# The first loads of a fused attention and MLP kernel reordered, and the taps of its convolution decoded one round later

## The chip, the cores and the metric

The kernel runs on one core of one Trainium2 chip. The metric is the device time of one execution in microseconds (us). PE is the matrix engine, DVE the vector engine, ACT the scalar engine, POOL GpSimd and SP the engine that issues nearly all DMAs; each works through its own instructions in order.

## What is computed

Three blocks follow each other: attention with features of exponentials, an MLP gated by a short convolution, and a second MLP with a low-rank mix along the sequence. B = 4, H = 8, S = 576, D = 64.

```python
def phi(x):                                   # w_phi: 64 x 128
    proj = np.einsum('bhsd,df->bhsf', x, w_phi)
    proj = proj - np.max(np.abs(proj), axis=-1, keepdims=True)
    return np.concatenate([np.exp(proj), np.exp(-proj)], axis=-1)
q_p, k_p = (phi(q), phi(k))
kv = np.einsum('bhsf,bhsd->bhfd', k_p, v); z = np.sum(k_p, axis=2)
num = np.einsum('bhsf,bhfd->bhsd', q_p, kv)
den = np.einsum('bhsf,bhf->bhs', q_p, z)[..., None] + 1e-06
x = num / den                                 # heads put side by side
h = np.maximum(x @ w_in, 0.0)
for k in range(3):                            # conv_w: 3 taps x 1024 channels
    conv_out += conv_w[k][None, None, :] * hp[:, k:k + S, :]   # hp: h, padded
x = h * (1.0 / (1.0 + np.exp(-conv_out))) @ w_out
u = x + low-rank mix of x                     # U, V
out = u + np.maximum(u @ w_ch1, 0.0) @ w_ch2
```

q, k, v and w_phi come as 32-bit floats; the taps `conv_w` and the MLP weights come as 64-bit floats and are decoded on the chip.

## The kernel before, in words

The attention stage runs in eight rounds (`NU`) of four heads each. A round's k and q come in three parts (g = 0 to 2). `centred` (line 256) projects a part with the weights `w2` into PSUM (`ppk`, `ppq`; a pool `ps_p` of two buffers), DVE takes the largest magnitude (`mk`, `mq`, line 266) and subtracts it (`dk`, `dq`, line 268). ACT then makes both exponentials (`ek`, lines 277 and 278). PE forms `kvp` (line 313) in two halves, u = 0 and u = 1, and the sums `zp`; q's features are transposed (`tq`) and exponentiated (`et`). The products `np` (line 381) and `dp` of a round are made during the next one, after ACT has copied `kv` (line 355).

The list `front` (line 480) is the order of a round. PE, DVE and ACT execute in exactly the order in which the code is written (`manual_schedule`); SP and POOL get an order from the tile scheduler. A lag of 1 or -1 in the list means that the step is for the next or the previous round; so `loads_kv` and `loads_q` load one round ahead.

Beside the attention each round decodes two pieces of the later weights (`win00`, `win01`, then `win10`, ...) from 64-bit floats in `split_steps`: a DMA into a staging tile `raw`, two DVE steps (lines 78 and 81), two ACT steps (87 and 89), two DVE steps (97 and 100), a POOL product (101), an ACT copy (171) and two POOL steps (172 and 173). The last of these, line 173, still reads `raw`. The pool `stage` (line 61) has two buffers for each of its tags `raw` and `x`.

The taps go the same way through `load_small` (line 104) at once: DMA, lines 78, 81, 87, 89, 97, 100, 101 and 125, and `load_cw` copies the result to `cw` (line 138). They are first used in the second stage, after 190 us. In the kernel before, `load_cw` is called ahead of the rounds, and its three DMAs gather single 8-byte values, since the taps lie in DRAM as 3 x 1024.

Ahead of all that, `ident` is built by POOL and eight warm-up products (line 230) run on it.

Of the kernel before, what the change touches and what calls it, by code (L numbers as in the profile page):

```python
# [8 lines left out]
F32 = mybir.dt.float32  # L9
# [3 lines left out]
AF = mybir.ActivationFunctionType  # L13
# [5 lines left out]
P = 128  # L19
# [5 lines left out]
def kernel(  # L25
# [15 lines left out]
    nc = tc.nc  # L41

    B, H, S, D = 4, 8, 576, 64
# [5 lines left out]
    NJ = FF // P  # L49
# [8 lines left out]
    cpool = ctx.enter_context(tc.tile_pool(name="cpool", bufs=1))  # L58
# [8 lines left out]
    cw = cpool.tile([P, 3 * NJ], F32, name="cw")  # L67
# [8 lines left out]
    def widen_head(raw, x):  # L76

        nc.vector.tensor_scalar(
            x, raw[:, :, 1], 3, 0x3FFFFFFF, op0=ALU.logical_shift_left, op1=ALU.bitwise_and
        )  # L80
        nc.vector.scalar_tensor_tensor(
            out=x, in0=raw[:, :, 1], scalar=-0x40000000, in1=x, op0=ALU.bitwise_and, op1=ALU.bitwise_or
        )

    def square_and_low(raw):
        high = raw.bitcast(F32)[:, :, 1]
        nc.scalar.activation(high, high, AF.Square)
        low = raw.bitcast(F32)[:, :, 0]
        nc.scalar.activation(low, raw.bitcast(U32)[:, :, 0], AF.Copy, scale=2.0**-52)

    def widen_rest(raw, x, mul_engine):


        low = raw.bitcast(F32)[:, :, 0]
        high = raw.bitcast(F32)[:, :, 1]
        xf = x.bitcast(F32)
        nc.vector.scalar_tensor_tensor(
            out=xf, in0=high, scalar=MIN_NORMAL_HI * MIN_NORMAL_HI, in1=xf, op0=ALU.is_ge, op1=ALU.mult
        )
        nc.vector.tensor_scalar(raw[:, :, 1], x, -0x800000, None, op0=ALU.bitwise_and)  # L100
        mul_engine.tensor_mul(low, low, high)
        return xf, low

    def load_small(p, n, name, parts, zero=()):

        wide = parts[0][2].dtype != F32
        x = stage.tile([P, 512], I32 if wide else F32, tag="x", name=f"{name}_x")[0:p, 0:n]
        if wide:
            raw = stage.tile([P, 512, 2], I32, tag="raw", name=f"{name}_raw")[0:p, 0:n, :]
        for z in zero:  # L110
            nc.gpsimd.memset(raw[:, z, :] if wide else x[:, z], 0)
        for r, c, src in parts:
            a = src.shape[1] if len(src.shape) == 3 else None
            if wide:
                d, s_ = raw[r, c, :], src.bitcast(I32)
                d = d.rearrange("p (a b) t -> p a (b t)", a=a) if a else d.rearrange("p b t -> p (b t)")
            else:
                d, s_ = x[r, c], src
                d = d.rearrange("p (a b) -> p a b", a=a) if a else d
            nc.sync.dma_start(out=d, in_=s_)  # L120
        if wide:
            widen_head(raw, x)
            square_and_low(raw)
            x, low = widen_rest(raw, x, nc.gpsimd)
            nc.vector.tensor_add(x, x, low)
        return x

    everything = slice(0, P)

    def load_cw():  # L130
        f = load_small(
            P, 3 * NJ, "cw",
            [
                (everything, slice(t * NJ, (t + 1) * NJ), conv_w[t : t + 1, :].rearrange("o (j p) -> p j o", p=P))
                for t in range(3)
            ],
        )
        nc.vector.tensor_copy(cw, f)

    def load_us(odd):  # L140
# [81 lines left out]
    G = 3  # L222
    GC = G * P

    w2 = cpool.tile([P, P], F32, name="w2")
    nc.sync.dma_start(out=w2[0:D], in_=w_phi)
    nc.sync.dma_start(out=w2[D:P], in_=w_phi)
    warm = ps_s.tile([P, 512], F32, tag="s", name="warm")
    for i in range(8):
        nc.tensor.matmul(warm[:, 0:P], lhsT=ident, rhs=ident, start=True, stop=True)  # L230
# [9 lines left out]
    def load_part(nm, src, i, g):  # L240
        t = fpool.tile([P, GC], F32, tag=f"{nm}r", name=f"{nm}r{i}_{g}", bufs=4)
        nc.sync.dma_start(out=t, in_=src[i, :, g * GC : (g + 1) * GC])
        raw[nm, i, g] = t

    def loads_kv(i):
        for g in range(G):
            load_part("k", k, i, g)
        t = fpool.tile([P, 10, 2, D], F32, tag="v", name=f"v{i}")
        nc.sync.dma_start(out=t.rearrange("p t h d -> p (t h d)"), in_=v[i])
        raw["v", i] = t  # L250

    def loads_q(i):
        for g in range(G):
            load_part("q", q, i, g)

    def centred(nm, i, g):
# [214 lines left out]
    def step(f, *args):  # L471
        return lambda i: f(i, *args)
# [4 lines left out]
    def second(i):  # L477
# [26 lines left out]
        (first, 0),  # L504
        (step(q_centred, 0), 0),
        (loads_kv, 1),
        (step(kv, 0), 0),
        (step(q_centred, 1), 0),
        (loads_q, 1),
        (step(turn_q, 0), 0),  # L510
        (step(q_features, 0), 0),
# [13 lines left out]
    ]  # L525

    loads_kv(0)
    loads_q(0)
    load_cw()
    att_order, rounds_order = ExitStack(), ExitStack()  # L530
    att_order.enter_context(tc.manual_schedule(engines={mybir.EngineType.PE}))
    rounds_order.enter_context(tc.manual_schedule(engines={mybir.EngineType.DVE, mybir.EngineType.Activation}))
    for i in range(NU):
        for step, lag in front:
            if 0 <= i + lag < NU:
                step(i + lag)
    rounds_order.close()
    i = NU - 1
    for _ in range(4):
# [191 lines left out]
    for n in range(B * NJ):  # L731
        b, j = divmod(n, NJ)
# [227 lines left out]
```

## Time and profile before

| | us |
|---|---|
| three runs, median (lowest, highest) | 830.88 (827.99, 832.11) |
| the profiled execution, device time | 833.57 |
| its span, first to last instruction | 831.5 |
| PE busy (share of the span) | 801.8 (96%) |
| DVE busy | 539.0 (65%) |
| ACT busy | 360.9 (43%) |
| POOL busy | 122.0 (15%) |
| mean granted TensorE clock | 0.989 of full |

Busy times are sums over the whole span; which engine limits a stretch is read from a table by stretches and from the waits in it. A granted clock of 1.00 is 2.4 GHz, 0.50 is 1.2 GHz. "Idle before <- X" in a row of a timeline names the event that ended an engine's idle time. The whole attention stage takes about the first 200 us.

### The profile page before, as it was taken

How to read it: one execution, taken by the hardware profiler on the slowest of the kernel's cores; microseconds unless marked ns; L12 is line 12 of the kernel's file. 1: busy time of each engine (PE TensorE's matmuls, PEld its weight loads, DVE VectorE, ACT ScalarE, POOL GpSimd, SP SyncE). 2: the span in 40 equal slices, each digit the busy share in tenths (PEclk: the TensorE clock that was granted, in tenths of full speed). 3: DMA queues.
4: the chain of work that ended last, by engine and by line, in shares of the span. 5: the costliest groups of instructions: out<-in, count | busy, mean ns of one | idle time of the engine just before them, and what ended most of it. 6: DMA issues, size and time to landing. Idle time of an engine off the chain costs nothing.

```text
span 831.5 us, 12728 instructions
## 1 busy us (share of the span) xinstructions
PE 801.8 (96%) x5092; PEld 647.1 (78%) x5092; DVE 539.0 (65%) x842; ACT 360.9 (43%) x642; POOL 122.0 (15%) x119
## 2 busy tenths in 40 slices
PE   5999999989989999999889999999999999999997
PEld 4666666657879888998668787888888888888886
DVE  3777777876799986985354596894378267231322
ACT  2777777776477664474311242442143132111110
POOL 0144444454331330000000000000000000000000
PEclk7999999999999999999999999999999999999999
DMA  7345555320312010111520221321031020000122
GB/s 209 129 126 170 170 170 170 110 81 2 94 52 102 26 58 26 39 52 38 178 89 1 63 58 45 100 70 34 1 102 51 1 68 34 0 1 1 68 84 76
DMA packets 39435, 61.27 MB, mean 74 GB/s; under 512 B 10257, under 2 KB 24721, under 8 KB 39377
## 3 DMA queue, kind: packets, MB, share of 16 engines
q1 hardware_dynamic: 39376, 60.46, 23.0%
q8 instruction: 40, 0.66, 0.3%
q14 instruction: 19, 0.15, 0.1%
HBM read 50.34 MB, written 10.04 MB: 73 GB/s over the span
## 4 chain that ended last, share of the span: by engine, by line
PE 83%; DVE 8%; DMA 4%; ACT 2%; issue 1%; SPq 1%; POOL 0%; DVEq 0%; ACTq 0%; POOLq 0%
PE po L856 22%; PE hps L834 22%; PE hp L590 10%; PE x2p L638 8%; PE kvp L313 4%; PE np L381 4%; PE ppq L263 2%; PE ppk L263 2%; PE zp L327 2%; PE tq L293 2%; PE dp L406 2%; DVE cv L602 1%; DVE xl L449 1%; PE x2m L654 1%; DMA c_5r<-in_moe_w_ch_dram 1%
## 5 line engine op out<-in xcount | busy, mean ns | idle before, releaser
L840 ACT ACTIVATE hh<-hps 128x512 fp32r<-128x512 f32 (+1 forms) x80 | 44.2, 553 | 214.2 <-PE hps L834 209.6
L841 DVE SCALAR_TENSOR_TENSOR hl<-hps,hh 128x512 fp32r<-128x512 f32 (+1 forms) x80 | 50.6, 633 | 99.2 <-ACT hh L840 99.0
L590 PE MATMUL hp<-xh,win 128*128 128x288 f32 x512 | 105.9, 297 | 0.5 <-ACT h L598 0.5
L638 PE MATMUL x2p<-wout,g 128*128 128x512 f32 x384 | 96.0, 392 | 2.1 <-DVE g L610 1.1
L834 PE MATMUL hps<-uh,c1h 128*128 128x512 f32 (+1 forms) x240 | 88.8, 370 | 1.1 <-ACT uh L796 1.1
L590 PEld LDWEIGHTS hp<-xh,win 128*128 128x128 f32 x512 | 85.1, 190 | 5.2 <-ACT h L598 0.7
L834 PE MATMUL hps<-ul,c1h 128*128 128x512 f32 (+1 forms) x240 | 88.5, 369 | 0.1
L834 PE MATMUL hps<-uh,c1l 128*128 128x512 f32 (+1 forms) x240 | 88.3, 368 | 0.0
L856 PE MATMUL po<-c2h,hh 128*128 128x512 f32 x216 | 84.9, 393 | 0.0
L856 PE MATMUL po<-c2l,hh 128*128 128x512 f32 x216 | 84.8, 393 | 0.0
L861 DVE TENSOR_TENSOR u<-u,po 128x512 f32<-128x512 f32 x90 | 58.5, 680 | 38.2 <-PE po L856 38.2
L856 PE MATMUL po<-c2h,hl 128*128 128x512 f32 x216 | 82.6, 392 | 0.0
L638 PEld LDWEIGHTS x2p<-wout,g 128*128 128x128 f32 x384 | 69.8, 188 | 15.9 <-DVE g L610 1.9
L590 PE MATMUL hp<-xl,win 128*128 128x288 f32 x256 | 76.6, 299 | 2.3 <-DVE xl L449 2.3
L602 DVE SCALAR_TENSOR_TENSOR cv<-h,cw,cv 128x576 f32<-128x576 f32 x64 | 53.3, 835 | 12.1 <-ACT cv L600 11.4
L631 POOL CAST ghold<-g 128x128 fp32r<-128x128 f32 x32 | 31.3, 983 | 155.9 <-DVE g L610 145.9
L834 PEld LDWEIGHTS hps<-uh,c1h 128*128 128x128 f32 x240 | 45.2, 188 | 9.1 <-ACT uh L796 1.3
L590 PEld LDWEIGHTS hp<-xl,win 128*128 128x128 f32 x256 | 48.7, 190 | 4.3 <-DVE xl L449 3.4
L834 PEld LDWEIGHTS hps<-ul,c1h 128*128 128x128 f32 x240 | 45.2, 188 | 8.3 <-DVE ul L797 0.5
L834 PEld LDWEIGHTS hps<-uh,c1l 128*128 128x128 f32 x240 | 45.2, 188 | 7.9
L856 PEld LDWEIGHTS po<-c2h,hl 128*128 128x128 f32 x216 | 41.0, 190 | 8.7
L856 PEld LDWEIGHTS po<-c2l,hh 128*128 128x128 f32 x216 | 41.0, 190 | 8.2
(488 smaller groups left out, 1500.5 us busy)
## 6 DMA issues: line engine op xcount, KB each, us to landing
v<-in_v_dram SPq DMA_DIRECT2D x8, 640.0 KB, 5.6
kr<-in_k_dram SPq DMA_DIRECT2D x24, 192.0 KB, 3.7
qr<-in_q_dram SPq DMA_DIRECT2D x24, 192.0 KB, 3.6
rb<-recd SPq DMA_DIRECT2D x32, 144.0 KB, 3.3
u<-x2d SPq DMA_DIRECT2D x18, 256.0 KB, 4.0
out_dram<-u SPq DMA_DIRECT2D x18, 256.0 KB, 2.1
x2d<-x SPq DMA_DIRECT2D x14, 256.0 KB, 2.3
c_0r<-in_moe_w_ch_dram SPq DMA_DIRECT2D x2, 512.0 KB, 4.2
```

The source lines that it names most:

```text
L263: nc.tensor.matmul(pp[:, s, c], lhsT=x[r, c], rhs=w2[r, :], start=True, stop=True)
L313: nc.tensor.matmul(o[s * D : (s + 1) * D, :], lhsT=raw["v", i][:, 5 * u + n, s, :], rhs=k_tile(i, s, 4 * u + n), start=(n == 0), stop=(n = ...
L381: nc.tensor.matmul(ps[r, 0:HC], lhsT=st["kv"][:, u, a, r], rhs=st["et"][:, s, a, cs], start=(a == 0), stop=(a == 1))
L590: nc.tensor.matmul(ps[:, 0:HC], lhsT=win[kk][:, wi, j * P : (j + 1) * P], rhs=xs[b][kk][xi][:, cs], start=(i == 0), stop=(i == 3 * NK - 1),)
L602: nc.vector.scalar_tensor_tensor(out=cv, in0=h[:, t : t + S], scalar=cw[:, t * NJ + j : t * NJ + j + 1], in1=cv, op0=ALU.mult, op1=ALU.add,)
L631: nc.gpsimd.tensor_copy(ghold[:, :, j, off : off + LEFT], g.bitcast(F32)[:, :, rest : rest + LEFT])
L638: nc.tensor.matmul(x2p[t], lhsT=g[:, gi, ts_], rhs=w[wi], start=(j == 0 and i == 0), stop=(j == NJ - 1 and i == 2),)
L834: nc.tensor.matmul(ps[:, 0:w], lhsT=ch[j, 0][wi][:, kc], rhs=x[:, kk, :], start=(n == 0), stop=(n == 3 * NK - 1))
L840: nc.scalar.activation(hh, ps[:, 0:w], AF.Relu)
L841: nc.vector.scalar_tensor_tensor(out=hl, in0=ps[:, 0:w], scalar=0.0, in1=hh.bitcast(F32), op0=ALU.max, op1=ALU.subtract)
L856: nc.tensor.matmul(po[i][t], lhsT=x[:, cs], rhs=w, start=(j == js[0] and n == 0), stop=(j == js[-1] and n == 2))
L861: nc.vector.tensor_add(u, u, p)
```

## The change

Four edits. The host writes `w_phi` twice below itself, so that one DMA, issued by ACT, fills `w2`; the host also lays the taps out as 128 x 24, so that one DMA of whole rows brings them. The first part of q is loaded ahead of v, in every round. A 128 x 1 tile of zeros goes through ACT's exponential at the beginning. And `load_cw` is called at the end of the first round's list instead of ahead of the rounds.

```diff
     def load_cw():
-        f = load_small(
-            P, 3 * NJ, "cw",
-            [
-                (everything, slice(t * NJ, (t + 1) * NJ), conv_w[t : t + 1, :].rearrange("o (j p) -> p j o", p=P))
-                for t in range(3)
-            ],
-        )
+        f = load_small(P, 3 * NJ, "cw", [(everything, slice(0, 3 * NJ), conv_w)])
         nc.vector.tensor_copy(cw, f)
...
     w2 = cpool.tile([P, P], F32, name="w2")
-    nc.sync.dma_start(out=w2[0:D], in_=w_phi)
-    nc.sync.dma_start(out=w2[D:P], in_=w_phi)
+    nc.scalar.dma_start(out=w2, in_=w_phi)
+    warm_exp = cpool.tile([P, 1], F32, name="warm_exp")
+    nc.gpsimd.memset(warm_exp, 0.0)
+    nc.scalar.activation(warm_exp, warm_exp, AF.Exp)
...
     def loads_kv(i):
         for g in range(G):
             load_part("k", k, i, g)
+        load_part("q", q, i, 0)
         t = fpool.tile([P, 10, 2, D], F32, tag="v", name=f"v{i}")
...
     def loads_q(i):
-        for g in range(G):
+        for g in range(1, G):
             load_part("q", q, i, g)
...
     loads_kv(0)
     loads_q(0)
-    load_cw()
...
         for step, lag in front:
             if 0 <= i + lag < NU:
                 step(i + lag)
+        if i == 0:
+            load_cw()
...
+        elif name == "w_phi":
+            a = _np.concatenate([a, a])
+        elif name == "moe_conv_w":
+            a = _np.ascontiguousarray(a.reshape(3, -1, 128).transpose(2, 0, 1)).reshape(128, -1)
```

DVE, from its first instruction on, in the kernel before. `mk0_1` is `mk` of round one (counted from 0 in names), part 1; the last number of a name is a running number.

```order
L266 TENSOR_REDUCE mk0_0_175<-ppk0_0_168 128x6
L268 TENSOR_TENSOR dk0_0_177<-ppk0_0_168,mk0_0_175 128x768
L78 TENSOR_SCALAR cw_x_150<-cw_raw_151 128x24
L81 SCALAR_TENSOR_TENSOR cw_x_150<-cw_raw_151,cw_x_150 128x24
L266 TENSOR_REDUCE mk0_1_189<-ppk0_1_182 128x6
L268 TENSOR_TENSOR dk0_1_191<-ppk0_1_182,mk0_1_189 128x768
L97 SCALAR_TENSOR_TENSOR cw_x_150<-cw_raw_151,cw_x_150 128x24
L100 TENSOR_SCALAR cw_raw_151<-cw_x_150 128x24
L266 TENSOR_REDUCE mk0_2_203<-ppk0_2_196 128x6
L125 TENSOR_TENSOR cw_x_150<-cw_x_150,cw_raw_151 128x24
L268 TENSOR_TENSOR dk0_2_205<-ppk0_2_196,mk0_2_203 128x768
L138 COPY cw_74<-cw_x_150 128x24
```

DVE at the end of round one and the beginning of round two, in the changed kernel (line numbers are those of the changed code).

```order
L263 TENSOR_REDUCE mq0_2_282<-ppq0_2_275 128x6
L265 TENSOR_TENSOR dq0_2_284<-ppq0_2_275,mq0_2_282 128x768
L97 SCALAR_TENSOR_TENSOR win00x_197<-win00r_196,win00x_197 128x512
L100 TENSOR_SCALAR win00r_196<-win00x_197 128x512
L78 TENSOR_SCALAR cw_x_327<-cw_raw_328 128x24
L81 SCALAR_TENSOR_TENSOR cw_x_327<-cw_raw_328,cw_x_327 128x24
L97 SCALAR_TENSOR_TENSOR cw_x_327<-cw_raw_328,cw_x_327 128x24
L100 TENSOR_SCALAR cw_raw_328<-cw_x_327 128x24
L125 TENSOR_TENSOR cw_x_327<-cw_x_327,cw_raw_328 128x24
L132 COPY cw_74<-cw_x_327 128x24
L263 TENSOR_REDUCE mk1_0_346<-ppk1_0_339 128x6
L265 TENSOR_TENSOR dk1_0_348<-ppk1_0_339,mk1_0_346 128x768
```

The six steps of the taps have moved from between round one's k parts to between `win00` and round two's first k part, now in one block.

SP in the kernel before, at the loads that it issues ahead for rounds two and three, with the semaphores that each waits for.

```order
L242 DMA qr2_0_509<-in_q_dram 128x384 [waits DMAHW7_49,PE_49]
L242 DMA kr2_1_481<-in_k_dram 128x384 [waits DMAHW0_49,PE_49]
L163 DMA win10r_430<-in_moe_w_in_dram 128x1024 [waits DMAHW1_49,DVE_49,Pool_49]
L242 DMA kr2_2_483<-in_k_dram 128x384 [waits DMAHW2_49,PE_49]
L242 DMA kr3_0_747<-in_k_dram 128x384 [waits DMAHW3_49,PE_49]
```

SP in the changed kernel, at the same place.

```order
L238 DMA qr2_0_485<-in_q_dram 128x384 [waits DMAHW3_49,PE_49]
L238 DMA kr2_1_481<-in_k_dram 128x384 [waits DMAHW4_49,PE_49]
L120 DMA cw_raw_328<-in_moe_conv_w_dram 128x48 [waits DMAHW5_49,DVE_49,Pool_49]
L157 DMA win10r_430<-in_moe_w_in_dram 128x1024 [waits DMAHW6_49,DMAHW5_49,DVE_49]
L238 DMA kr2_2_483<-in_k_dram 128x384 [waits DMAHW7_49,PE_49]
```

The load of the taps stands where that of `win10` stood and waits for DVE and POOL as that did; `win10` stands behind it and waits for the taps. ACT's two steps for the taps stand between its copy of `zt` and its copy of `kv`, and POOL's product behind line 173 (line 167 of the changed code) of `win00`. PE's order is the same in both kernels.

## Rows read from the trace of the kernel before

**Rows 1.** The page, busy time, share of the span and instructions of PE.

```profile
PE 801.8 (96%) x5092; PEld 647.1 (78%) x5092; DVE 539.0 (65%) x842; ACT 360.9 (43%) x642; POOL 122.0 (15%) x119
```

**Rows 2.** Stretches: us, busy of each engine, granted clock, DMA share, GB/s.

```profile
8.50:29.80 21.30, 14.03 (x136) 9.03 (x132) 12.13 (x20) 11.18 (x17) 0.23 (x1) 0.76 0.70 210
29.80:51.20 21.40, 21.40 (x244) 13.96 (x240) 16.67 (x23) 15.82 (x29) 7.15 (x6) 1.00 0.40 125
```

**Rows 3.** Timeline of PE, 0 to 30 us: start, us, instructions, idle before.

```profile
1.47 3.43 PE L230 MATMUL warm<-ident 128*128 128x128 f32 x16 [1.47 <-POOL ones L235]
4.82 1.61 PE L263 MATMUL ppk<-w,kr 64*128 64x128 f32 x24
7.86 0.94 PE L263 MATMUL ppk<-w,kr 64*128 64x128 f32 x12 [1.43 <-DVE dk L268]
16.07 1.65 PE L263 MATMUL ppq<-w,qr 64*128 64x128 f32 x12 [7.27 <-DVE dk L268]
17.65 4.23 PE L313 MATMUL kvp<-ek,v 128*64 128x256 f32 x20
21.81 0.94 PE L263 MATMUL ppq<-w,qr 64*128 64x128 f32 x12
...
23.49 2.38 PE L313 MATMUL kvp<-ek,v 128*64 128x256 f32 x20
```

**Rows 4.** Timeline of all engines, 0 to 30 us: loads and the taps.

```profile
0.74 0.60 SPq L226 DMA_DIRECT2D w<-in_w_phi_dram  x1
...
5.48 6.26 SPq L120 DMA_DIRECT2D cw_raw<-in_moe_conv_w_dram  x3
...
6.80 0.96 DVE L268 TENSOR_TENSOR dk<-ppk,mk 128x768 f32<-128x768 f32 x1
...
13.67 1.28 ACT L89 ACT_TABLE_LOAD   x1 [13.67 <-DMA cw_raw<-in_moe_conv_w_dram]
13.71 0.18 DVE L78 TENSOR_SCALAR cw_x<-cw_raw 128x24 int32<-128x24 int32 x1 [5.95 <-DMA cw_raw<-in_moe_conv_w_dram]
...
14.97 0.23 ACT L89 ACTIVATE cw_raw<-cw_raw 128x24 f32<-128x24 uint32 x1
...
17.43 0.23 POOL L101 TENSOR_TENSOR cw_raw<-cw_raw 128x24 f32<-128x24 f32 x1 [15.79 <-DVE cw_raw L100]
```

**Rows 5.** Stretches of 1 us in the front, columns as in rows 2.

```profile
9.80:10.80 1.00, 0.00 (x0) 0.00 (x0) 0.00 (x0) 0.00 (x0) 0.00 (x0) 1.00 0.81 89
...
12.80:13.80 1.00, 0.00 (x0) 0.00 (x0) 0.09 (x1) 0.13 (x1) 0.00 (x0) 0.50 1.01 201
```

**Rows 6.** Timeline of all engines, 28 to 60 us: round two begins.

```profile
29.77 0.94 PE L263 MATMUL ppk<-w,kr 64*128 64x128 f32 x12
...
30.00 1.04 POOL L101 TENSOR_TENSOR win00r<-win00r 128x512 f32<-128x512 f32 x1 [12.35 <-ACT et L302]
...
30.75 0.96 DVE L266 TENSOR_REDUCE mk<-ppk 128x6 f32<-128x768 f32 x1 [0.88 <-PE ppk L263]
...
31.78 0.38 PE L362 MATMUL pz<-ident,zt 128*128 128x128 f32 x2
...
32.35 1.29 POOL L173 TENSOR_TENSOR win<-win00x,win00r 128x512 fp32r<-128x512 f32 x1
...
33.67 0.33 SPq L163 DMA_DIRECT2D win10r<-in_moe_w_in_dram  x1
...
34.18 0.94 PE L263 MATMUL ppk<-w,kr 64*128 64x128 f32 x12
```

**Rows 7.** DMA issues of the whole run: count, KB each, median us to landing.

```profile
w<-in_w_phi_dram SPq DMA_DIRECT2D x2, 32.0 KB, 2.1
cw_raw<-in_moe_conv_w_dram SPq DMA_DIRECT2D x3, 8.0 KB, 5.8
us_raw<-in_moe_U_dram SPq DMA_DIRECT2D x2, 16.0 KB, 3.3
```

**Rows 8.** Answer for the tile `cw_raw`: landing of its three loads.

```profile
DMA to landing us min/median/max: 5.1/5.8/6.8
```

## The prediction

> **What bounds the kernel now.** I read the engines' busy times first: PE is busy 801.8 of 831.5 us [rows 1], so time can only be won where PE stands still or runs slowly. Then the stretches by round of the attention stage: from round two on PE is busy through all of its 21.4 us at full clock, while in the first 30 us it is busy for 14.0 of 21.3 us at a mean granted clock of 0.76 [rows 2]. The change touches only this front, so what matters is when round two begins and at what pace; everything behind is a chain that moves as a block.
>
> The PE timeline of the front shows the hole: after the third group of k it stands idle for 7.27 us, until 16.07, released by a `dk` of DVE [rows 3]. DVE itself stood: its instruction for the taps (`cw_x`, line 78) begins at 13.71, 5.95 us after it was free, because the three loads of the taps had been issued from 5.48 on and took until then [rows 4]. The hole has a second price: the granted clock is still 1.00 at 9.8 to 10.8, but 0.50 (1.2 GHz) at 12.8 to 13.8 [rows 5]. The first group of q therefore takes 1.65 us where the next takes 0.94, and the first half of `kvp` 4.23 us where the second takes 2.38 [rows 3]: 0.71 + 1.85 = 2.56 us.
>
> **Part 1: w in one load on ACT's queue, k first on SP's.** SP gets rid of two issues of 0.6 us [rows 4], and k comes 1.2 us earlier. This buys nothing: the eight warm-up products run from 1.47 to 4.90, and the first group of k starts right there, at 4.82 [rows 3]. They wait for the identity, which POOL builds; POOL gets one more memset before it, so I add 0.1 us. If this cover were gone, the parts together could give up to 1.2 us.
>
> **Part 2: an exponential of zeros.** It draws the 1.28 us table load to the beginning [rows 4], beside the warm-up products. In the kernel before that load ran while DVE was still in `mk` and `dk`, and PE waited for `dk`: no gain. In the changed kernel it keeps 1.28 us off the first exponentials; these are needed by `kvp` at about 10.8, and even 1.28 us later they would end at 7.9 + 1.28 + 1.6 = 10.8. Zero either way.
>
> **Part 3: first q ahead of v.** The first q is needed at 9.9, v at 10.8; by then both are issued and landed in either order (all loads of round one are issued by some 4 us instead of 5.4). Zero.
>
> **Part 4: the taps leave the front.** The DVE order has `mk` and `dk` of the second k part directly behind those of the first. `dk` begins at 6.80 and takes 0.96 [rows 4]; with 0.1 of delay and two more steps of 0.98 the second `dk` ends at 9.85, and the first group of q starts at 9.9 instead of 16.07: 6.15 us. From there PE has no gap: each later DVE step is done when PE comes to it (the first `dq` ends at 13.8, its transposes start at 13.97). Without the long idle I take the clock to stay up, as it did through the 1.43 us wait at 7.86 [rows 3, 5]: another 2.56 us. Round two's first group of k then starts 8.7 us earlier, at 21.1 instead of 29.77 [rows 6].
>
> **Part 5: the taps come back at the end of round one.** This is the step that decides. Only two staging buffers exist for raw data, and both are taken by `win00` and `win01`. The taps' load needs the buffer of `win00`, so SP waits until POOL has done its last step on it: line 173, which ends at 32.35 + 1.29 = 33.64, 3.87 us after round two's first group of k began at 29.77 [rows 6]. In the kernel before it is `win10` that waits there, needed by nobody soon: it is issued at 33.67 [rows 6]. Now it is the taps, and DVE, which works in written order, stands in front of them with `mk` and `dk` of round two behind; ACT too, with the copy of `kv` behind. This chain keeps its distances whatever the front does, because POOL's last step hangs on DVE's line 100 and that on round one's last `dq`.
>
> The length of the wait. The transfer is not in the trace in this shape (128 rows of 192 B). Nearest rows: 2.1 us for the 32 KB halves of w, 3.3 us for the 16 KB pieces of `us_raw`, 5.8 us for the old loads of the taps in 8-byte pieces [rows 7]. I take 2.2, for w has whole rows as the new load has, and keep 1.8 to 3.8 for the range. The Trainium skill, page "DMA: Bandwidth & Descriptors", section on the anatomy of one DMA, puts a DMA at a fixed 2.0 us plus bytes over 436 GB/s (fitted on GpSimd's path), an estimate of 2.06 us for 24.6 KB; the sum would be 0.14 us better by it. The trace agrees for w (2.1) and not for the smaller `us_raw` (3.3).
>
> Counted from round two's first group of k: issue at 3.9, landed at 6.1, then the decode, one step behind the other: six DVE steps of 0.18 to 0.2 us, an ACT step of 0.2 and a POOL step of 0.23 with two hand-overs [rows 4], 1.9 us. DVE is free for `mk` at 8.0 (before: 0.98), `dk` ends at 9.97, and the second group of k starts at 10.05; before it started at 34.18, which is 4.41 [rows 6]. **Loss: 5.64 us.** PE can do `np` meanwhile, but first ACT has to pass its two steps for the taps and copy `kv`: 6.1 + 0.4 (DVE) + 0.4 + 0.6 + 0.2 = 7.7. PE's last work before that is `pz`, which ends 2.4 us after the first group of k [rows 6], so it stands idle for some 5.3 us. In the front the clock had fallen within 3 us of idling (from 8.80; 1.00 until 10.8) [rows 5], so I expect it to fall here and to take about the same 2.56 us from the first `np` and the group behind it. From then on PE is full again as in rounds two to eight: DVE works 16.7 of 21.4 us there [rows 2] and catches up.
>
> **The sum.** Gain 6.15 + 2.56 = 8.7; loss 5.64 + 2.56 = 8.2. Net 0.5 us faster: 833.57 - 0.5 = 833.1 against the profiled execution (its span is 831.5), and 830.9 - 0.5 = **830.4 us** against the median of 830.88, which the profiled run exceeds by 2.7.
>
> **Rivals.**
> - The clock holds in the second gap: it is 2 us shorter than the first, and `np` comes in between. Then 2.56 us more are won: 827.8. For it: 5.3 against 7.27 us idle. Against it: the fall within 3 us.
> - The clock falls in the front as well: PE works in single groups with waits of about 1 us between them until 10.8. Then 2.56 us less: 832.9. Against it: the clock stayed at 1.00 through and after such a wait at 6.4 to 8.8.
> - The change does what it says, with no wait in place of the old one: the load would find its buffer free and the decode (1.9 us from 0.1 on) would end before `mk` delays PE. Then all of the 8.7 us stay: 822.2. Against it stand the order of SP, where the load waits for DVE and POOL, and the two buffers; it needs a buffer that I have not seen.
> - Slower: the taps' load lands as late as it did before although it is whole rows, because small pieces and not bytes set its time. Each us goes straight into DVE's wait, and from 2.75 us on the changed kernel is the slower one. At 5.8 us it gives 830.4 + 3.6 = 834.0, at 6.8 (the slowest old one [rows 8]) 835.0; over 0.5% is reached from 6.9 us. Against it: 1024 pieces each before, 128 now.
>
> **How the numbers follow.** About 0.5% (4.2 us) is what a measurement of this kernel can tell from no change; the three runs before spread from 828.0 to 832.1. Chances: forecast 0.50, clock holds 0.17, clock falls twice 0.14, no wait 0.07, late load 0.07, and 0.05 for a shift of clock or transfers later in the kernel. The range takes in the first three with the transfer's 1.8 to 3.8 us: 826.3 to 833.8. Faster by over 0.5% is the case without a wait and some of the rest: 0.09. Slower by over 0.5%: the late load together with a clock that falls twice, and some of the rest: 0.06. Same: 0.85.
>
> **What will show it.** Right, if the changed trace has the first group of q near 10 us, the first half of `kvp` near 2.4 us, round two's first group of k near 21, then a DVE wait for the DMA of the taps of about 6 us, a PE idle of about 5 us before `np`, a granted clock of 0.50 behind it, and the second group of k of round two at about 33.7 (21.1 + 10.05 + 2.5). Wrong, if DVE does not wait at line 78 at all, if the load takes over 4 us, if the warm-up products end elsewhere than near 4.9, or if rounds three to eight are no longer 21.4 us.

## The result, and the profile after

The changed kernel takes **836.17 us** (median of 6 runs, 834.96 to 839.0), the kernel before 830.82 on the same chip (6 runs): a ratio of 1.0071, 95% interval 1.0048 to 1.0094. It is slower by 0.7%. The forecast was 830.4 us, the range ended at 833.8, and "slower" had been given 0.06: the prediction is **wrong**, by 5.8 us, on the wrong side.

The front, on which the whole prediction was spent, is not where it went wrong. PE's timeline of the changed kernel, 0 to 36 us (start, us, instructions, idle before), against [rows 3, 6]:

```profile
1.50 3.79 PE L226 MATMUL warm<-ident 128*128 128x128 f32 x16 [1.50 <-POOL ones L231]
5.21 2.06 PE L260 MATMUL ppk<-w,kr 64*128 64x128 f32 x24
...
10.56 0.94 PE L260 MATMUL ppq<-w,qr 64*128 64x128 f32 x12 [0.92 <-PE ppk L260]
11.43 2.38 PE L310 MATMUL kvp<-ek,v 128*64 128x256 f32 x20
...
21.69 0.94 PE L260 MATMUL ppk<-w,kr 64*128 64x128 f32 x12
...
28.61 4.11 PE L378 MATMUL np<-et,kv 128*64 128x288 f32 x16 [4.53 <-ACT kv L352]
32.65 1.32 PE L260 MATMUL ppk<-w,kr 64*128 64x128 f32 x12
```

The first group of q stands at 10.56 instead of 16.07, the first half of `kvp` takes 2.38 us instead of 4.23, and round two begins at 21.69 instead of 29.77: 8.08 us early. Then PE stands for 4.53 us before `np`, `np` takes 4.11 us (the next one, at 33.91, takes 2.16), and the second group of k comes at 32.65 instead of 34.18. What PE waited for is in the timeline of the other engines at that place, which answers to [rows 6] and [rows 4]:

```profile
24.39 1.28 POOL L167 TENSOR_TENSOR win<-win00x,win00r 128x512 fp32r<-128x512 f32 x1
25.69 0.33 SPq L120 DMA_DIRECT2D cw_raw<-in_moe_conv_w_dram  x1
27.27 0.18 DVE L78 TENSOR_SCALAR cw_x<-cw_raw 128x24 int32<-128x24 int32 x1 [5.48 <-DMA cw_raw<-in_moe_conv_w_dram]
...
29.18 0.95 DVE L263 TENSOR_REDUCE mk<-ppk 128x6 f32<-128x768 f32 x1
```

POOL's last step on `win00` frees the buffer, SP issues the taps at 25.69, they are there at 27.27, and DVE has stood 5.48 us. The granted clock follows the idling (stretches, columns as in [rows 2]):

```profile
24.00:25.00 1.00, 0.08 (x1) 0.00 (x0) 0.00 (x0) 0.00 (x0) 0.92 (x2) 1.00 0.34 124
26.00:27.00 1.00, 0.00 (x0) 0.00 (x0) 0.00 (x0) 0.00 (x0) 0.00 (x0) 0.83 0.13 25
28.00:29.00 1.00, 0.39 (x2) 0.29 (x4) 0.49 (x3) 1.00 (x3) 0.23 (x1) 0.50 0.00 0
...
43.10:64.50 21.40, 21.40 (x241) 13.96 (x242) 17.04 (x22) 15.97 (x28) 10.37 (x8) 1.00 0.48 155
```

From round two's second group of k on, DVE's instructions stand 1.15 us earlier than the same ones before (34.03 against 35.17, and still 160.19 against 161.34), and still 1.45 earlier at 411 us. So up to there the change has won a little more than the 0.5 us forecast.

The loss comes after that, in the last stage, the second MLP. Same DVE instructions, before and after: 489.57 and 489.12 (-0.45), 583.82 and 584.61 (+0.79), 657.56 and 659.36 (+1.80), 751.26 and 754.54 (+3.28), 808.62 and 812.76 (+4.14), the spans 831.5 and 835.7 (+4.2). From 411 us on it is 5.6 us, and no single event but a drift. The page's first row shows where it lies; compare [rows 1]:

```profile
PE 808.3 (97%) x5092; PEld 647.6 (77%) x5092; DVE 536.6 (64%) x842; ACT 361.8 (43%) x643; POOL 120.7 (14%) x120
```

PE executes the same 5092 products and is busy 6.5 us longer. It waits for nobody there, and its clock is not lower: the stretch from 600 to 830 us of the changed kernel has PE busy throughout at a granted clock of 1.00.

```profile
600.00:830.00 230.00, 230.00 (x1064) 190.47 (x1063) 103.76 (x177) 45.20 (x79) 0.00 (x0) 1.00 0.12 42
```

The kernel before has the same clock there (its last product ends at about 827 us):

```profile
600.00:830.00 230.00, 227.29 (x1061) 190.20 (x1059) 104.07 (x177) 45.17 (x79) 0.00 (x0) 1.00 0.13 44
```

What differs is the pace of single products. The chain of waits of the changed kernel, 600 to 660 us, in order of time (start, us, line, number of products):

```profile
609.91 2.72 PE hps L832 x12
612.63 1.36 PE po L854 x6
...
618.07 2.72 PE po L854 x12
620.78 2.80 PE hps L832 x12
623.59 2.75 PE po L854 x12
...
637.40 2.80 PE hps L832 x12
```

and of the kernel before:

```profile
619.68 2.72 PE hps L834 x12
622.40 2.72 PE po L856 x12
...
636.00 2.72 PE hps L834 x12
```

Twelve products of 512 columns take 2.72 us before (227 ns each) and, after, sometimes 2.72 and sometimes 2.80 (233 ns). The groups of instructions by shape say which ones (busy us, mean ns of one; a mean includes the overlap with the next product, so it is larger than the pace, but its difference is the same). The changed kernel:

```profile
L854 PE MATMUL po<-c2h,hl 128*128 128x512 f32 x216 | 82.8, 393 | 0.0
L832 PE MATMUL hps<-uh,c1h 128*128 128x512 f32 x192 | 76.3, 397 | 1.1 <-ACT uh L794 1.1
...
L854 PE MATMUL po<-c,hh 128*128 128x512 f32 x144 | 43.8, 396 | 0.0
```

and the kernel before:

```profile
L856 PE MATMUL po<-c2h,hl 128*128 128x512 f32 x216 | 82.6, 392 | 0.0
L834 PE MATMUL hps<-uh,c1h 128*128 128x512 f32 x192 | 75.3, 392 | 1.1 <-ACT uh L796 1.1
...
L856 PE MATMUL po<-c,hh 128*128 128x512 f32 x144 | 43.0, 390 | 0.0
```

`po` with the weights `c` is 6 ns slower per product, `hps` with `c1h` 5 ns, `po` with `c2h` hardly. The code says what distinguishes them: SBUF is given out from two ends. `xcpool` (weights `c1`, `c2`) and the pool `left` (`uh` of the first block, `hh`, `hl`) lie on the left side, above `cpool`; `wpool` (weights `c`) and the pool `right` (`uh` of later blocks) hang from the right end. A 512-column product of `hps` streams `uh` against one of these weights, one of `po` streams the weights against `hh` or `hl`, so each product reads two tiles of SBUF. A product of `c` and `hh` takes one operand from each side, one of `c2h` and `hh` takes both from the left. The change adds one tile to `cpool`, `warm_exp`, of 4 bytes per partition, for which 32 are set aside. In the compiled program all that lies on the left above it is 32 bytes per partition higher than before, and the right side is where it was.

### The profile page after: what moved, and what is told of

It is laid out like the page before. It is cut to its first block, busy times and chain, and to the rows that moved or that the text cites. A ratio compares the mean times of both kernels' runs of the same rounds, so it can differ in the third digit from the quotient of the medians.

```text
span 835.7 us, 12727 instructions
## 1 busy us (share of the span) xinstructions
PE 808.3 (97%) x5092; PEld 647.6 (77%) x5092; DVE 536.6 (64%) x842; ACT 361.8 (43%) x643; POOL 120.7 (14%) x120
## 4 chain that ended last, share of the span: by engine, by line
PE 83%; DVE 8%; DMA 4%; ACT 2%; issue 1%; POOL 1%; SPq 0%; DVEq 0%; ACTq 0%; POOLq 0%
PE po L854 22%; PE hps L832 22%; PE hp L588 10%; PE x2p L636 8%; PE kvp L310 4%; PE np L378 4%; PE ppk L260 2%; PE ppq L260 2%; PE tq L290 2%; PE zp L324 2%; PE dp L403 2%; DVE cv L600 1%; DVE xl L446 1%; PE x2m L652 1%; DMA c_5r<-in_moe_w_ch_dram 1%
## 5 line engine op out<-in xcount | busy, mean ns | idle before, releaser
L854 PEld LDWEIGHTS po<-c2h,hh 128*128 128x128 f32 x216 | 41.0, 190 | 8.6
```

Source lines behind the costliest of these rows:

```text
L854: nc.tensor.matmul(po[i][t], lhsT=x[:, cs], rhs=w, start=(j == js[0] and n == 0), stop=(j == js[-1] and n == 2))
```

## The experiments

Three batches, each compared with runs of the kernel before beside it (medians 831.17, 830.68 and 831.38 us). "Pace" is worked out from the traces: the mean distance from start to start of successive 512-column products between 540 and 830 us. It is 227.0 ns before and 230.6 ns after. Each kernel was profiled once, so a pace is that of one execution.

### Which part of the change costs it: sp_w, no_exp, before_spare, pad64

**sp_w** undoes the move of the load of w to ACT's queue.

```diff
-    nc.scalar.dma_start(out=w2, in_=w_phi)
+    nc.sync.dma_start(out=w2, in_=w_phi)
```

> The changed kernel with w loaded by SP's queue (one load) instead of ACT's. Placement theory: still about 836 (the front starts at most 0.5 us later or not at all, the warm-up covers it). Queue theory: the last stage at 227 ns and about 830.

Measured: 837.87 us, ratio 1.0076 [1.0053, 1.01], pace 230.6. The queue has nothing to do with it.

**no_exp** leaves out the exponential of zeros, and with it the tile.

```diff
-    warm_exp = cpool.tile([P, 1], F32, name="warm_exp")
-    nc.gpsimd.memset(warm_exp, 0.0)
-    nc.scalar.activation(warm_exp, warm_exp, AF.Exp)
```

> The changed kernel without the tile of zeros and its exponential. Placement theory: 829.7 plus 0 to 1.3 us for the table load, which then stands before the first exponential; last stage at 227 ns. Queue and timing theory: 836.

Measured: 829.83 us, 0.9978 [0.9956, 1.0], pace 227.0. Everything else of the change is still there, the loss is gone.

**before_spare** is the kernel before with an unused tile at the place where the change puts its own.

```diff
+    spare = cpool.tile([P, 1], F32, name="spare")
+    nc.gpsimd.memset(spare, 0.0)
```

> The kernel before, with one unused 4-byte tile set to zero behind w2, nothing else. Placement theory: about 837 us (830.8 plus the 6.5 us that the changed kernel loses behind the front), 231 ns a pass on average in the last stage. Queue and timing theory: 831, as before.

Measured: 835.45 us, 1.0057 [1.0038, 1.0075], pace 230.6. A tile that nobody reads costs 4.3 us; the exponential is not needed for it, nor anything that the change moves in time. The theory of the place in memory stands; that the tile's own write costs the time is excluded only by before_spare256 below.

**pad64** makes the changed kernel's tile 64 bytes, on the thought that products want tiles on a line of 64.

```diff
-    warm_exp = cpool.tile([P, 1], F32, name="warm_exp")
+    warm_exp = cpool.tile([P, 16], F32, name="warm_exp")[:, 0:1]
```

> The changed kernel, its tile of zeros 64 bytes wide instead of 4. Placement theory (the 4-byte tile moves every later tile of the left side of SBUF by 32 bytes against the right side, and products whose two operands lie 32 bytes apart modulo 64 take about 233 instead of 227 ns a pass): the offset is a full 64 again, the last stage goes at 227 ns, about 829.7 us (before minus the 1.15 us that the front gained). Queue theory (ACT's use of a DMA queue slows the last stage) and timing theory (the shifted schedule does): 836 as the changed kernel.

Measured: 836.65 us, 1.0072 [1.0046, 1.0098], pace 230.6. Missed: a shift by 64 is as bad as one by 32, so that theory of the place fell.

### What about the place: pad128, both64, pad256, both128, before_spare256

Three readings were left: another line size; the two operands must lie alike, at the same distance from some line; or every shift costs. **pad128** and **pad256** differ from pad64 in the tile's width alone (`[P, 32]`, `[P, 64]`). **both64** and **both128** also put a spare tile of the same size at the right end, so that the right side moves down as far as the left moves up:

```diff
+    rpad = ctx.enter_context(tc.tile_pool(name="rpad", bufs=1, side="right"))
+    right_spare = rpad.tile([P, 16], F32, name="right_spare")
+    nc.gpsimd.memset(right_spare, 0.0)
     wpool = ctx.enter_context(tc.tile_pool(name="wpool", bufs=8, side="right"))
```

> The changed kernel with the tile of zeros 128 bytes wide. 64 bytes did not bring the pace back, so the placement theory is narrowed: products are slow when their operands do not lie alike modulo 128 (or 256). Modulo 128: last stage back at 227 ns a pass, about 830 us. Modulo 256 or a larger block: 231 ns and 836. If not the place but the tile itself slows the kernel (one more write of POOL and one more exponential of ACT at the start): 836 with any width.

> The changed kernel with the tile of zeros 64 bytes wide and 64 bytes taken from the right side too, so that both sides lie at 32 modulo 128 (they differ by 128 modulo 256). If only the distance of the two operands counts (modulo 128): 227 ns, about 830 us. If the place itself counts (96 modulo 128 is the good one): 231 ns or more, 836 or more. If the block is 256: 231 ns and 836.

> The changed kernel with the tile of zeros 256 bytes wide and nothing else. 128 bytes left the last stage slow and two other kernels with 256 had it fast, so the placement theory is now: operands must lie alike modulo 256. It expects 227 ns a pass and 829.9 us (831 minus the 1.15 us of the front). If those two were fast for another reason (their taps do not wait at the end of round one): 836.

> The changed kernel with 128 bytes for the tile of zeros on the left side and 128 taken from the right, so that both sides lie at 96 modulo 256 (before: both at 224). If only the distance of the two operands counts: 227 ns a pass and about 830 us. If the place itself counts: 231 ns and 836 or more.

**before_spare256** is the kernel before with the unused tile of 256 bytes.

```diff
+    spare = cpool.tile([P, 64], F32, name="spare")[:, 0:1]
+    nc.gpsimd.memset(spare, 0.0)
```

> The kernel before with the unused tile 256 bytes wide instead of 4. Placement theory modulo 256: 831, as before, 227 ns a pass. If an extra tile or its write at the start slows the kernel by itself: 836, as with 4 bytes.

Measured, with the addresses that the compiled programs give to `c1`, `c2`, `hh` (left) and to `c` (right), modulo 256 bytes per partition:

| kernel | left | right | pace, ns | us | ratio, 95% interval |
|---|---|---|---|---|---|
| before | 224 | 224 | 227.0 | 830.8 | 1 |
| after, sp_w, before_spare | 0 | 224 | 230.6 | 836.2, 837.9, 835.5 | 1.0071 [1.0048, 1.0094] (after) |
| pad64 | 32 | 224 | 230.6 | 836.65 | 1.0072 [1.0046, 1.0098] |
| pad128 | 96 | 224 | 230.1 | 838.69 | 1.0087 [1.0054, 1.0119] |
| both64 | 32 | 160 | 230.1 | 836.6 | 1.0068 [1.0044, 1.0091] |
| pad256 | 224 | 224 | 227.0 | 832.21 | 0.9996 [0.9973, 1.0019] |
| before_spare256 | 224 | 224 | 227.0 | 830.51 | 0.9996 [0.998, 1.0011] |
| both128 | 96 | 96 | 227.0 | 831.49 | 1.0 [0.998, 1.002] |

Only the kernels in which left and right lie alike modulo 256 are at the old pace. both64, alike modulo 128 only, is slow, so 128 is not enough; both128, where neither side lies where it lay before, is at the old pace, so the place itself does not matter. The groups by shape show it for the mixed pair in both64

```profile
L857 PE MATMUL po<-c,hh 128*128 128x512 f32 x144 | 43.7, 395 | 0.0
```

and in both128:

```profile
L835 PE MATMUL hps<-uh,c1h 128*128 128x512 f32 x192 | 75.3, 392 | 1.1 <-ACT uh L797 1.1
...
L857 PE MATMUL po<-c,hh 128*128 128x512 f32 x144 | 43.0, 390 | 0.0
```

Within the changed kernel the pairs tell the same, pace against before by median: `po<-c,hh` (right with left) 234 against 227 ns, `po<-c2h,hh` (left with left) 227 against 227. So does a single group: in `hps<-uh,c1h` the first block takes `uh` from the left, as `c1h`, and its 512-column products follow each other at 228.6 ns in the mean, those of the later blocks, with `uh` from the right, at 233.5; before, all of them at 227.8.

The traces also say when the time goes. From the same DVE instruction at 430 us to the end of the span, the kernels whose sides do not lie alike lose 4.1 to 5.3 us against the kernel before (after 5.3, sp_w 4.9, before_spare 4.7, pad64 4.8, pad128 4.1, both64 4.9), while no_exp, pad256, both128, before_spare256 and the three kernels of the next part stay within 0.3 us of it.

pad256 differs from no_exp in the front, too. After single waits of about 1 us its granted clock was 0.55 from 11 to 12 us and 0.50 from 12 to 14 (1.00 in the changed kernel), and the first group of q and the first half of `kvp` took

```profile
10.82 1.44 PE L260 MATMUL ppq<-w,qr 64*128 64x128 f32 x12 [0.92 <-PE ppk L260]
12.19 3.50 PE L310 MATMUL kvp<-ek,v 128*64 128x256 f32 x20
```

instead of 0.94 and 2.38 us; in no_exp they took 0.94 and 2.38.

### What the front was worth: front_cw, own_cw, own_cw2

With the place mended, the remaining question was the prediction's own: what does the taps' wait cost, and can the 8 us be kept? All three kernels keep left and right alike (a tile of 256 bytes, or tiles of 512 together).

**front_cw** issues and decodes the taps ahead of the rounds, through the first free staging buffer.

```diff
     loads_q(0)
+    load_cw()
...
-        if i == 0:
-            load_cw()
```

> The changed kernel with load_cw back ahead of the rounds (one load of whole rows), the tile of zeros 256 bytes wide so that all places are alike. My theory of the front: the load lands 1.6 us after its issue at about 4, before DVE needs it, so DVE does not wait and only its six small steps (about 1.2 us) lie in the chain to the first group of q; no second wait, no fall of the clock: round two's second group of k near 27.3 instead of 34.18, 831.0 - 6.9 = 824.1. Rival (any decode between the first parts of k stalls DVE on ACT and POOL too, some 3 us): 826 or more.

Measured: 831.75 us, 1.001 [0.9991, 1.0029]; missed. Its timeline, front:

```profile
4.01 0.63 SPq L120 DMA_DIRECT2D cw_raw<-in_moe_conv_w_dram  x1
...
10.19 0.18 DVE L78 TENSOR_SCALAR cw_x<-cw_raw 128x24 int32<-128x24 int32 x1 [10.19 <-DMA cw_raw<-in_moe_conv_w_dram]
...
12.55 1.65 PE L260 MATMUL ppk<-w,kr 64*128 64x128 f32 x12 [5.56 <-issue]
```

The same load that took 1.58 us from issue to use in the changed kernel takes 6.2 here, behind the loads of q and v. DVE stands in front of it, PE idles 5.56 us and comes back at half clock (1.65 us for a group of 0.94). This is the rival "late load", met at another place. The pieces are the same in both kernels; the traffic is not: the DMA engines are busy for 0.94 of the 6.2 us here and for 0.09 of the 1.58 us there. own_cw, below, issues the load at the same place, and there it takes 6.5 us. So the time of this load goes with what is under way around it, as far as these three cases show.

**own_cw** gives the taps staging tiles of their own and issues the load there too, but decodes at the end of round one.

```diff
+    cw_x = cpool.tile([P, 3 * NJ], I32, name="cw_x")
+    cw_raw = cpool.tile([P, 3 * NJ, 2], I32, name="cw_raw")
     def load_cw():
-        f = load_small(P, 3 * NJ, "cw", [(everything, slice(0, 3 * NJ), conv_w)])
-        nc.vector.tensor_copy(cw, f)
+        x, raw = cw_x, cw_raw
+        widen_head(raw, x)
+        square_and_low(raw)
+        x, low = widen_rest(raw, x, nc.vector)
+        nc.vector.tensor_add(x, x, low)
+        nc.vector.tensor_copy(cw, x)
...
     loads_q(0)
+    nc.sync.dma_start(out=cw_raw.rearrange("p b t -> p (b t)"), in_=conv_w.bitcast(I32))
```

> The changed kernel with staging tiles of their own for the taps, loaded in round one, POOL's product given to DVE, and the total of new tiles a multiple of 256 bytes. My theory: the wait at the end of round one is only the wait for the shared buffer, so it is gone; the decode (about 1.7 us) fits into the time before PE needs round two's second part; round two's second group of k near 26.1 instead of 34.18: 831.0 - 8.1 = 822.9 us. Rival (the wait is DVE's own backlog at the end of the round and not the buffer): 829 to 830, as the kernel without the tile of zeros.

Measured: 828.21 us (823.97 to 832.09), 0.997 [0.9945, 0.9995]. The wait for the DMA is gone, but only part of the gain came. DVE's and PE's timeline at the place:

```profile
22.30 0.70 DVE L97 SCALAR_TENSOR_TENSOR cw_x<-cw_raw,cw_x 128x24 f32<-128x24 f32 x1 [0.32 <-ACT cw_raw L87]
...
23.04 1.20 DVE L100 TENSOR_SCALAR cw_raw<-cw_x 128x24 int32<-128x24 int32 x1
...
24.35 1.27 DVE L101 TENSOR_TENSOR cw_raw<-cw_raw 128x24 f32<-128x24 f32 x1
...
28.00 0.94 PE L267 MATMUL ppk<-w,kr 64*128 64x128 f32 x12 [1.93 <-issue]
```

and POOL's, on `win00`:

```profile
21.93 1.04 POOL L101 TENSOR_TENSOR win00r<-win00r 128x512 f32<-128x512 f32 x1 [20.24 <-ACT win L172]
22.93 1.28 POOL L173 TENSOR_TENSOR win00x<-win00x,win 128x512 f32<-128x512 f32 x1
24.28 1.29 POOL L174 TENSOR_TENSOR win<-win00x,win00r 128x512 fp32r<-128x512 f32 x1
```

Three of the small DVE steps take 0.70, 1.20 and 1.27 us instead of 0.18. Each begins while a step of POOL is under way and ends 0.03 to 0.05 us after that step (23.00 after 22.97, 24.24 after 24.21, 25.62 after 25.57); the next two, behind POOL's last, take 0.18 again. The decode takes 4.4 us, `mk` and `dk` of round two stand behind it, and PE idles 1.93 us.

**own_cw2** moves only the decode, to a place in round two where DVE's two steps for the next group of k are already done.

```diff
         (step(k_centred, 1), 0),
+        (lambda i: load_cw() if i == 1 else None, 0),
...
-        if i == 0:
-            load_cw()
```

> As the kernel with staging tiles of their own for the taps, but decoded inside round two behind the second part of k, where POOL stands idle and DVE waits for PE. In the first form the seven DVE steps took 4.4 us instead of 1.7, beside POOL's steps for the first weight piece, and PE stood idle for 1.9 us. Expected: no PE idle at round two's second group of k, which starts near 26.1 (before: 34.18); all of 8.1 us gained in the rounds against 6.2 in the first form, so 823 by the sum, and 826 if the executions lose behind the rounds what those of the first form lost (its median was 828.2 for 824.5 by the sum). Rival (the small DVE steps are slow wherever they stand): PE idle again, 828.

Measured: **823.65 us** (821.15 to 825.23, 4 runs), 0.9902 [0.9879, 0.9926], pace 227.0: about 1% faster than the kernel before and, by medians of different batches, 12.5 us faster than the changed one. The timeline shows the decode in pieces of 0.18 and PE without a gap there:

```profile
26.68 2.16 PE L385 MATMUL np<-et,kv 128*64 128x288 f32 x16
28.66 0.17 DVE L78 TENSOR_SCALAR cw_x<-cw_raw 128x24 int32<-128x24 int32 x1
28.77 0.94 PE L267 MATMUL ppk<-w,kr 64*128 64x128 f32 x12
...
29.56 0.18 DVE L100 TENSOR_SCALAR cw_raw<-cw_x 128x24 int32<-128x24 int32 x1
29.64 2.15 PE L410 MATMUL dp<-et,z 128*32 128x288 f32 x32
```

Its DVE instructions stand 8.15 us earlier than before at 143 us and 8.53 at 776: what the front wins is kept to the end. Against own_cw the new place of the decode is worth 2.0 us by the traces (own_cw's DVE instructions stand 6.18 us earlier at 143 us). The 4.6 us between the two medians are more than that, from different batches, and the two profiled executions both took 824.73 us: own_cw's won 1.8 us between 411 and 430 us. There, at the beginning of the last stage, PE waits for DVE (2.2 to 4.1 us in the traces), and the executions differ by up to 2.2 us from the kernel before, whatever the change: the granted clock from 424 to 430 us is 0.72 in the profile of the kernel before and 0.59 in sp_w's, and own_cw's stays at 1.00 from 412 to 436 us.

## Why the prediction was wrong, step by step

- **The step that failed** is the first one: "everything behind is a chain that moves as a block". The order of work behind does move as a block; its pace does not stay. Part 2 costed the exponential of zeros at "zero either way" by looking at its instructions only. It left out that it brings a tile, and that a tile at the bottom of the left side moves every tile above it. The missing term measures 4.3 us by before_spare (835.45 - 831.17), 5.3 by the drift in the trace from 430 us on. The kernels without that shift, no_exp at 0.9978 and pad256 at 0.9996, land where the forecast had put the change: within 0.5%.
- **Part 1, zero: right.** PE's first group still begins where the warm-up products end, at 5.21 instead of 4.82. The warm-up itself took 3.79 instead of 3.43 us, so the 0.1 us of delay became 0.39. Why the warm-up is longer is not shown; it took 3.78 us in no_exp too.
- **Part 2's timing, zero: right**, but not as it was reasoned. The exponential of zeros runs at 2.46, its table load from 1.17 beside the warm-up. In no_exp, without it, the table load runs from 1.17 too, long before the first exponential (8.15): once the taps are out of the front, the exponential of zeros keeps no 1.28 us off anything. No gain from it shows in the times either: with it and the place mended 832.21, without it 829.83, in different batches.
- **Part 3, zero: right.** No engine waited for q or v in the front.
- **Part 4, 8.7 us: right**, 8.08 measured: 5.51 to the first group of q and 2.6 from the clock (`ppq` 0.94 for 1.65, `kvp` 2.38 for 4.23). The 0.6 us short of the forecast come from the first two groups of k, which end 0.84 us later than before (5.21 + 2.06 against 4.82 + 1.61) where 0.1 had been allowed. The clock holds through single waits of about 1 us in this execution. In that of pad256 it did not (its rows stand with the experiment), and the rounds ended 0.71 us later than before instead of 1.15 earlier. The rival "the clock falls in the front as well" thus comes true in some executions.
- **Part 5, loss 5.64 + 2.56: right in mechanism**, and each link of it is in the trace: line 167 of POOL, SP's issue 4.0 us after the first group of k, DVE's wait of 5.48, PE's idle of 4.53 (forecast 5.3), clock 0.50 behind it. The transfer was taken as 2.2 us and took 1.58 from issue to use. By the Trainium skill, page "DMA: Bandwidth & Descriptors", section on the anatomy of one DMA, the estimate had been 2.06 us (a fixed 2.0 us and the bytes, fitted on GpSimd's path); the measurement decides, and lies 0.5 us below it. The net gain of 1.15 us instead of 0.5 is the difference of two errors: the gain came out 0.6 us smaller, the loss 1.3 smaller (8.08 - 1.15 = 6.9 for 8.2), and the shorter transfer is about half of the latter.
- **The rivals.** "The clock holds in the second gap" did not happen. "No wait" came true only in own_cw2, which gave 823.65 against the 822.2 worked out for it. The 0.05 for "a shift of clock or transfers later in the kernel" was the only place where the true case could have hidden, and it named the wrong resources. The range does not follow from its own terms, either: the fastest of its three cases with a transfer of 1.8 us gives 827.8 - 0.4 = 827.4, the slowest with 3.8 us 832.9 + 1.6 = 834.5, and not 826.3 and 833.8; the 836.17 lies outside both.
- **The test that the prediction set** for its own failure did point there, in part: it asked whether rounds three to eight keep 21.4 us. They do. It should have asked the same of the last stage, which is half of the time. One of its signs of being wrong showed, and had nothing to do with the loss: the warm-up products ended at 5.29 and not near 4.9.

**What stays open.** Which part of the memory or of PE makes the rule of 256 bytes isn't shown; the runs show only that pace goes with the distance of the two operands. The stages before 430 us show no clear loss. `x2p` has both operands on the right and stays at 392 ns in both kernels, as the rule has it. Shorter products are another matter: those of `hps` with 256 columns take `c1h` from the left and `uh` from the right, like the slow ones with 512, and take what they took before. Before, then after:

```profile
L834 PE MATMUL hps<-uh,c1h 128*128 128x256 f32 x48 | 13.5, 282 | 0.0
L832 PE MATMUL hps<-uh,c1h 128*128 128x256 f32 x48 | 13.5, 282 | 0.0
```

`hp` (288 columns, `win` on the right, `xh` on the left) stays at 297 ns in the mean; there half of the products have their operands 128 bytes apart modulo 256 in the kernel before already, since they read `xh` from 1152 bytes on, and the median from start to start is 131 to 134 ns, alike or not, in both kernels. So the rule is shown for 512 columns alone; why shorter products do not follow it is open. That POOL's steps hold up DVE's small ones in own_cw rests on their ends, which fall together, and on own_cw2, where the two are apart; POOL's steps were not taken out by themselves.

## What to carry to other kernels

A new tile is not free because nobody waits for it: look at which tiles it moves, and compare the pace of single products far behind the edit (equal clock, equal count, longer busy time) before looking for a wait. When a load moves, cost it by what is under way where it is issued, and when a small step moves, by which engine works beside it there. If a wait moves on instead of going, as this one of 5 to 6 us did, give its data a buffer of their own and put the consumer where its engine has slack.

## What was not expected of the hardware

- Products of 128x512 follow each other at about 227 ns when their two tiles in SBUF lie alike modulo 256 bytes per partition, and at about 233 when they don't (distances of 32, 64, 128, and 128 after moving both sides by 64): some 5 us on 836. Products of 256 columns show no difference (282 ns in the rows both times).
- Small DVE steps of 0.18 us took 0.70 to 1.27 us beside POOL's steps on a 128x512 tile, and ended within 0.05 us of the end of POOL's step (own_cw).
- A load of 128 rows of 192 B was usable 1.58 us after its issue with little else under way (DMA engines busy 0.09), and 6.2 us after it behind the loads of q and v (front_cw, busy 0.94).
- In the gap of 4.53 us before `np` PE's granted clock was 1.00 over 24 to 25, 0.83 over 26 to 27 and 0.50 (1.2 GHz) when the work came back at 28.61; it was 0.50 still from 31 to 32, 0.75 from 33 to 34 and 1.00 from 35 to 36.
